# Skip weights of a state-space convolution put into PSUM by TensorE, and a rounding constant put into the instruction

## The chip, the cores and the metric

The kernel runs on one core of one Trainium2 chip. The metric is the device time of one execution in microseconds. Before the change the median of three runs is 1748.3 us (1747.56 to 1751.75). One further execution was profiled; its span, from the first to the last instruction, is 1749.5 us. The engines are called PE (TensorE matmul), PEld (TensorE weight load), DVE (VectorE), ACT (ScalarE), POOL (GpSimd) and SP (SyncE, which here only issues DMAs).

## The reference, cut to what matters

A layer norm with modulation feeds a diagonal state-space convolution, whose result, with a skip term, is added to the input; then a gated MLP follows, which the change does not touch.

```python
def _A_ref(u, A_re, A_im, B_re, B_im, C_re, C_im, log_dt, Dskip):   # L = 2048, D = 576, N = 128
    dt = exp(log_dt)[:, None]
    logdA = dt * (A_re + 1j * A_im);  dB = dt * (B_re + 1j * B_im);  Cc = C_re + 1j * C_im
    P = exp(logdA[:, :, None] * l[None, None, :])
    K = einsum("dn,dnl,dn->dl", Cc, P, dB).real
    y = irfft(rfft(u, 2L) * rfft(K, 2L))[:L] + u * Dskip
x = x + ga * _A_ref(h, ...)          # h: layer norm of x, modulated by c
x = x + gb * _B_ref(h2, ...)         # MLP with a spatial gate
```

The skip term `u * Dskip` is the same as adding `Dskip` to the kernel `K` at lag 0. The kernel before does it in that way.

## The kernel before, in words

The function `ssm` does the convolution part, `Mlp` the rest. The 576 channels are cut into 36 groups of 16 channels. For each group g these units make the convolution kernel in the frequency domain:

- `e_unit` (L442): TensorE makes logarithms of magnitudes in PSUM, ACT takes Exp of them (L449 two banks, L452 one bank) into the tile `et`.
- `t_unit` (L456): TensorE makes phases (L465). For g below NR = 10 TensorE also adds and takes away the rounding constant MAGIC (L469) and DVE copies the result (L477). For the other 26 groups ACT writes phase + MAGIC (L480, `Identity` with the per-partition column `magic` of the tile `consts_s` as bias) and DVE takes the rounded phase from the phase (L481). Then DVE takes the absolute value of the result (L482). All of it is in the tile `ft`.
- `s_unit` (L485): two Sin on ACT (L487, L488), in place.
- `p_unit` (L490): four DVE products of magnitudes and sines (L498 to L501) into `pg` and `et`.
- `kg_unit` (L504): 32 group products on TensorE (L511), 128 x 32 weights against 64 columns, four channels side by side in the four quarters of the output partitions, into one PSUM bank (`pk`, four of them in rotation); ACT copies the bank's 256 columns to the tile `kab` (L514).
- `d_unit` (L516): DVE adds the skip weights of the group to column 63 of each of the four 64-column pieces of `kab` (L518; 128 partitions x 4). The skip weights lie in the tile `dsk`, 4 columns for each group, with a number in partitions 0, 32, 64 and 96 and zeros elsewhere.
- `k1_unit` (L520): eight matmuls (L528) turn `kab` with the constant `r1`, ACT (L535) or DVE (L533) copies the result to `k1`.

When a chunk of 128 channels is complete, `u_unit` (L574: matmul L578, copy L579, two DMAs on POOL L580 and L581), `z_unit` (L584: matmuls L590, DVE product L591), `v_unit` (L594: matmuls L598 and L599, copy L600, DMA L601) and `y_unit` (L637: matmuls L644, DVE add L646, DMA L647) convolve it with the layer-normed input `u`.

The layer norm itself is done early: `ln_load`, `ln_stats` (L389; for the last two of four row blocks with `bn_stats` into the tile `bs`), `ln_rows` (L414) and `ln_half` (L423: matmuls L431, copies to `st1o` L433, which has two buffers, and a DMA on POOL to `u_d` L434). The constant matrices `r1`, `fwd`, `inva`, `invb` and `ones` are views of one tile `small`, which is loaded at the start by SP. The DRAM array `c_small` holds seven 128 x 128 matrices, of which the first is the identity; the kernel before skips it here.

The order: in the early part `early_steps` (L674) records units in the order of a long string, one letter for a unit and a number for its group; from group 9 on, a loop of ticks (L735) records one step of each unit for each tick, in the order of one of three strings (L756). ACT, and after the letters V and T also DVE and TensorE, are not bound to that order: a scheduler moves instructions within each engine. So a change of one unit also moves others. SP and POOL are queues in order.

## Time and profile before

The whole program is bound by TensorE in the MLP (after about 440 us); the convolution, where the change lies, is the first 440 us. Busy time by stage, from the view of busy time by stretch, in us:

| stretch | PE | DVE | ACT | POOL | granted clock |
|---|---|---|---|---|---|
| 0 to 44 | 11.73 | 32.66 | 28.52 | 19.07 | 1.00 |
| 175 to 219 | 43.07 | 41.15 | 42.34 | 14.59 | 0.94 |
| 394 to 438 | 29.68 | 36.89 | 20.74 | 9.68 | 0.84 |
| whole span, 1749.5 | 1654.4 | 1256.1 | 834.3 | 250.5 | 0.982 |

How to read it: an engine that is busy for nearly the whole of a stretch may be what bounds it; in the stretches of 43 or 44 us between 175 and 350 us three engines are, at once. The chain of waits (the work that ended last, followed back) then says which of them set the pace, piece by piece. Matmul ends are modelled in these profiles, so a busy PE need not be PE at its limit. A float32 matmul stands in the trace as two records: 32 group products of one group are 64 records.

### The profile page before, as it was taken

To read this page: it belongs to the slowest core of one execution; us is meant where nothing else is said; L and a number is where in the kernel's file an instruction comes from. 1 tells how busy PE (TensorE), PEld (TensorE's weight loads), DVE (VectorE), ACT (ScalarE), POOL (GpSimd) and SP (SyncE) were. 2 spreads that over 40 slices of the span, in tenths; PEclk is the share of its full clock that TensorE was granted. 3 is DMA by queue.
4 is the path that set the end of the run, shared out by engine and by line. 5 is a ranking of instruction groups with operands and counts; after the bars stand their busy time and mean duration, and the time that the engine had idled before them with its cause. 6 is when DMAs were issued, how large, how long until landed. Compare 5 with 4: busy or idle time off the path is not lost.

```text
span 1749.5 us, 36390 instructions
## 1 busy us (share of the span) xinstructions
PE 1654.4 (95%) x15174; PEld 1241.1 (71%) x15174; DVE 1256.1 (72%) x2259; ACT 834.3 (48%) x1121; POOL 250.5 (14%) x412
## 2 busy tenths in 40 slices
PE   2788999996999999999999999999999999999999
PEld 1344666664455446777878888888888888888887
DVE  7876999948999997888898767797444387334432
ACT  6877999834677665445443433343221233122210
POOL 4421332342122110000000000000111100111100
PEclk9897999998999999999999999999999999999999
DMA  8477656798698798777656887764766563556531
GB/s 227 136 223 229 187 155 170 207 271 248 215 292 272 222 249 290 258 253 261 221 193 205 289 290 263 241 231 138 246 219 231 195 224 106 194 197 208 193 110 41
DMA packets 182934, 376.24 MB, mean 215 GB/s; under 512 B 39105, under 2 KB 102977, under 8 KB 182001
## 3 DMA queue, kind: packets, MB, share of 16 engines
q1 hardware_dynamic: 138304, 168.50, 31.9%
q0 software_dynamic: 37984, 178.55, 31.2%
q10 hardware_dynamic: 6480, 26.86, 3.8%
q8 instruction: 119, 1.95, 0.5%
q14 instruction: 47, 0.38, 0.1%
HBM read 263.11 MB, written 101.31 MB: 208 GB/s over the span
## 4 chain that ended last, share of the span: by engine, by line
PE 32%; issue 28%; DVE 18%; DMA 4%; POOL 3%; ACT 2%; SPq 0%; POOLq 0%; ACTq 0%; DVEq 0%
PE ps L152 28%; POOL zset L1906 2%; DMA zset<-set_d 2%; DVE bsz L152 2%; DVE zset L152 1%; DVE n L152 1%; DVE gt L152 1%; DVE rq L152 1%; DVE wsp L152 1%; PE pk L578 1%; PE pk L598 1%; PE pk L590 1%; DVE pg L499 1%; DVE wso L152 1%; DVE ft L481 1%
## 5 line engine op out<-in xcount | busy, mean ns | idle before, releaser
L152 PEld LDWEIGHTS <-zset 128*128 128x128 f16 x7182 | 701.9, 98 | 92.6 <-DVE zset L152 7.6
L152 PE MATMUL ps<-wsp,zset 128*128 128x256 f16 x6048 | 667.7, 273 | 7.2 <-DVE zset L152 5.8
L152 PE MATMUL pz<-wz,nt 128*128 128x512 f16 (+1 forms) x1120 | 221.9, 358 | 9.0 <-DVE nt L152 4.3
L152 ACT ACTIVATE z<-gt 128x1024 f16<-128x1024 f32 x56 | 59.0, 1054 | 287.0 <-DVE gt L152 287.0
L152 PEld LDWEIGHTS <-nt 128*128 128x128 f16 x1120 | 109.1, 98 | 115.7 <-DVE nt L152 5.8
L1906 POOL DMA_DIRECT2D zset<-set_d x96 | 50.8, 529 | 869.1 <-PE ps L152 619.7
L152 DVE SCALAR_TENSOR_TENSOR gt<-ps,sc,bsp 128x512 f32<-128x512 f32 x36 | 27.0, 750 | 205.5 <-PE ps L152 203.8
L152 PE MATMUL ps<-wout,z 128*128 128x288 f16 x1344 | 170.0, 286 | 0.0
L152 PEld LDWEIGHTS <-z 128*128 128x128 f16 x1344 | 131.5, 98 | 33.0
L152 PE MATMUL ps<-n2o,zset 128*128 128x256 f16 x1134 | 128.2, 273 | 0.0
L152 DVE SCALAR_TENSOR_TENSOR gt<-ps,sc,gt 128x512 f32<-128x512 f32 (+1 forms) x180 | 122.2, 696 | 7.6
L152 DVE TENSOR_TENSOR raw<-raw 128x512 f32<-128x512 f32 (+2 forms) x228 | 119.2, 528 | 11.2 <-DMA raw<-z_d 6.9
L152 ACT ACTIVATE zset<-raw 128x1792 f16<-128x1792 f32 x48 | 81.2, 1691 | 58.3 <-PE ps L152 25.3
L152 DVE TENSOR_TENSOR zset<-raw,zset 128x1792 f16<-128x1792 f32 x48 | 97.0, 2020 | 15.9 <-ACT zset L152 15.9
L152 DVE TENSOR_TENSOR z<-ps,z 128x512 f32<-128x512 f32 (+1 forms) x126 | 72.0, 599 | 36.8 <-ACT z L152 26.7
L152 ACT ACTIVATE wsp<-raw,sc 128x1792 f16<-128x1792 f32 x25 | 44.6, 1785 | 42.7 <-DVE raw L152 35.0
L152 ACT ACTIVATE z<-z,sc 128x1024 f32<-128x1024 f32 x21 | 24.1, 1148 | 75.6 <-DVE z L152 71.9
L152 ACT ACTIVATE z<-pz,sc 128x512 f32<-128x512 f32 (+1 forms) x96 | 52.0, 582 | 16.2 <-DMA z_d<-z 9.8
L152 PE MATMUL ps<-n2q,wf 128*128 128x512 f16 x252 | 55.7, 379 | 0.0
L152 ACT ACTIVATE z<-z,nm,r 128x1152 f32<-128x1152 f32 x24 | 31.5, 1342 | 49.7 <-DVE nm L152 29.3
L152 PE MATMUL ps<-wout,z1b 128*128 128x288 f16 x384 | 52.6, 286 | 0.5 <-ACT z1b L152 0.5
L152 DVE SCALAR_TENSOR_TENSOR wsp<-raw,sc,wsp 128x1792 f16<-128x1792 f32 x25 | 51.9, 2078 | 0.0
(345 smaller groups left out, 2452.7 us busy)
## 6 DMA issues: line engine op xcount, KB each, us to landing
zset<-set_d POOLq DMA_DIRECT2D x96, 896.0 KB, 4.9
raw<-z_d SPq DMA_DIRECT2D x48, 512.0 KB, 5.5
set_d<-zset ACTq DMA_DIRECT2D x24, 896.0 KB, 5.9
z_d<-z POOLq DMA_DIRECT2D x32, 576.0 KB, 9.7
zset<-wa_d POOLq DMA_DIRECT2D x18, 896.0 KB, 4.9
raw<-in_w_spT SPq DMA_DIRECT2D x25, 512.0 KB, 4.4
set_d<-zset SPq DMA_DIRECT2D x12, 896.0 KB, 5.5
u_d<-st1o POOLq DMA_DIRECT2D x16, 576.0 KB, 4.8
```

What stands on the lines that cost most here:

```text
L152: return self.tc.keep_in_program_order(f(*a, **k))
L481: V.scalar_tensor_tensor(f, f, MAGIC, pa, op0=ALU.subtract, op1=ALU.subtract)
L499: V.tensor_tensor(pr, pi, c3[:, :, None, :].to_broadcast([128, 16, 2, 32]), op=ALU.mult)
L578: T.matmul(pm, fwd, u1, start=True, stop=True)
L590: T.matmul(pm[:, w * j:w * j + w], cst[k // 8][:, k % 8], k1t[c][:, k, :w], start=True, stop=True)
L598: T.matmul(pm, inva, zz[:, 0], start=True, stop=False)
L1906: self.nc.gpsimd.dma_start(o, self.set_d[f, j - 1] if j else self.wa_d[f])
```

## The change

Three edits:

1. `d_unit` goes. In its place `kg_unit` begins with four matmuls: the columns of the identity that belong to a quarter of the partitions (128 x 32 weights) against the group's four columns of `dsk`, written to columns 63, 127, 191 and 255 of the bank. They start the accumulation; all group products then accumulate onto them. The identity comes from the first matrix of `c_small`, so `small` has seven matrices in place of six, and its load 128 x 896 numbers in place of 128 x 768. The letters d go from the order strings.
2. L480 becomes `Copy` with the constant MAGIC as a number in the instruction.
3. `bs` has one buffer in place of two.

```diff
-        small = cp.tile([128, 6, 128], F32, name="small")
-        r1 = [small[:, 0], small[:, 1]]
-        fwd, inva, invb, ones = (small[:, i] for i in range(2, 6))
+        small = cp.tile([128, 7, 128], F32, name="small")
+        eye = small[:, 0]
+        r1 = [small[:, 1], small[:, 2]]
+        fwd, inva, invb, ones = (small[:, i] for i in range(3, 7))
...
-                bs = ep.tile([128, 4, 2, 6], F32, name="bs")
+                bs = ep.tile([128, 4, 2, 6], F32, name="bs", bufs=1)
...
-                A.activation(f, pa, AF.Identity, bias=magic)
+                A.activation(f, pa, AF.Copy, bias=MAGIC)
...
         def kg_unit(g):
             pr, pi, gr, gi = tt.pop(g)
             pm = ps1()
+            for j in range(4):
+                rows = slice(32 * j, 32 * j + 32)
+                T.matmul(pm[rows, 63:256:64], eye[:, rows], dsk[:, 4 * g:4 * g + 4], start=True, stop=False, skip_group_check=True)
             for i in range(4):
-                for x_, y_, st in ((gr, pr, True), (gi, pi, False)):
+                for x_, y_, st in ((gr, pr, False), (gi, pi, True)):
                     for j in range(4):
                         c = 4 * i + j
                         T.matmul(pm[32 * j:32 * j + 32, 64 * i:64 * i + 64], x_[:, c], y_[:, c].rearrange("p s j -> p (s j)"),
-                                 start=st, stop=not st, skip_group_check=True)
+                                 start=False, stop=st, skip_group_check=True)
...
-        def d_unit(g):
-            kk = kab[g]
-            V.tensor_tensor(kk[:, :, 63], kk[:, :, 63], dsk[:, 4 * g:4 * g + 4], op=ALU.add)
...
-                    q.dma_start(small, I["c_small"][:, 128:].rearrange("p (i c) -> p i c", i=6))
+                    q.dma_start(small, I["c_small"].rearrange("p (i c) -> p i c", i=7))
...
-            for n in ('kpt1svyzdeeu', 'ktespy1dzvu', 'ktvsdzuyp1')[tick % 3]:
+            for n in ('kpt1svyzeeu', 'ktespy1zvu', 'ktvszuyp1')[tick % 3]:
```

In the whole program DVE has 36 instructions fewer (all of them L518), TensorE 144 matmuls more, and ACT 33 table loads in place of 35. Behind the convolution no instruction stands elsewhere than before. Within it the scheduler moves many. Three places:

ACT in the early part, from the Sin of a group and the layer norm's statistics to the Exp of three groups, before:

```order
L488 ACTIVATE ft<-ft 128x1024
L452 ACT_TABLE_LOAD
L452 ACTIVATE et<-pk 128x512
L218 ACTIVATE pt<-t_ph 128x432
L433 ACTIVATE st1o<-ps 128x576 x2
L487 ACT_TABLE_LOAD
L487 ACTIVATE ft<-ft,consts_s 128x1024
L220 ACTIVATE pt<-t_sq_609 128x432
L433 ACTIVATE st1o<-ps 128x576 x2
L488 ACTIVATE ft<-ft 128x1024
L449 ACT_TABLE_LOAD
```

and now (line numbers are up to three higher, L514 has become L518, and the copy to `k` is still L535):

```order
L489 ACTIVATE ft<-ft 128x1024
L221 ACTIVATE pt<-t_sq_478 128x432
L401 ACTIVATE st1o,ss<-ln_x,nm 128x576
L488 ACTIVATE ft<-ft,consts_s 128x1024
L489 ACTIVATE ft<-ft 128x1024
L219 ACTIVATE pt<-t_ph 128x432
L434 ACTIVATE st1o<-ps 128x576 x2
L518 ACTIVATE kab<-pk 128x256
L221 ACTIVATE pt<-t_sq_613 128x432
L535 ACTIVATE k_923<-pk 128x32x16
L434 ACTIVATE st1o<-ps 128x576 x2
L450 ACT_TABLE_LOAD
```

The single Exp that stood between two groups' Sin has moved to the Exp before them, so two table loads are gone here. A second such pair is gone a little later, and one new pair has come, ahead of six copies to `st1o`:

```order
L535 ACTIVATE k_923<-pk 128x32x16
L453 ACT_TABLE_LOAD
L453 ACTIVATE et<-pk 128x512
L372 ACTIVATE gar<-ps 128x576
L434 ACTIVATE st1o<-ps 128x576 x6
L518 ACTIVATE kab<-pk 128x256
L434 ACTIVATE st1o<-ps 128x576
L488 ACT_TABLE_LOAD
```

DVE in the steady part, the products of two groups (`pg`, `et`) with the phases (`ft`) of others between them, before:

```order
L498 TENSOR_TENSOR pg<-et,ft 128x1024
L499 TENSOR_TENSOR pg<-et,ft 128x1024
L481 SCALAR_TENSOR_TENSOR ft<-ft,ps 128x1024
L500 SCALAR_TENSOR_TENSOR et<-ft,et 128x16x32
L501 TENSOR_TENSOR et<-ft,et 128x16x32
L482 TENSOR_SCALAR ft<-ft 128x1024
L591 TENSOR_TENSOR zz<-pk,uu 128x1024
L518 TENSOR_TENSOR kab<-kab,dsk 128x4
L498 TENSOR_TENSOR pg<-et,ft 128x1024
```

and now:

```order
L499 TENSOR_TENSOR pg<-et,ft 128x1024
L500 TENSOR_TENSOR pg<-et,ft 128x1024 x2
L501 SCALAR_TENSOR_TENSOR et<-ft,et 128x16x32
L502 TENSOR_TENSOR et<-ft,et 128x16x32
L482 SCALAR_TENSOR_TENSOR ft<-ft,ps 128x1024
L533 COPY k_1934<-pk 128x32x16
L483 TENSOR_SCALAR ft<-ft 128x1024
L591 TENSOR_TENSOR zz<-pk,uu 128x1024
L499 TENSOR_TENSOR pg<-et,ft 128x1024
```

The addition L518 is gone; one product of the next group stands ahead of the phase subtraction (now L482), which has moved back behind it and behind the two `et` products.

On TensorE the four new matmuls (L510) stand right ahead of the first group products (L515, before L511). On POOL the six DMA issues of the last pole table (`pa_d`) now stand ahead of the second write of `u_d`, which stood ahead of them; one DMA issue changes places with its neighbours in the steady part, and two reads of `u_d` on SP stand behind a load of MLP weights in place of ahead of it.

4 lines of the change are left out of this document (2 added, 2 removed), and 6 rows, old and new, of the table T.

## The prediction

> **What bounds the kernel now.** Behind 440 us nothing moves, so only the convolution counts, and the question is whether it ends earlier. I read first the view of busy time by stretch (from and to, length, then busy us of PE, PEld, DVE, ACT and POOL with their instructions, granted clock, DMA share, GB/s):
>
> ```profile
> 0.00:44.00 44.00, 11.73 (x49) 4.52 (x50) 32.66 (x107) 28.52 (x55) 19.07 (x36) 1.00 0.86 228
> ...
> 219.00:262.00 43.00, 42.00 (x642) 25.84 (x631) 42.34 (x54) 42.10 (x58) 14.84 (x26) 1.00 0.55 155
> 262.00:306.00 44.00, 43.40 (x656) 27.09 (x655) 42.82 (x55) 41.28 (x56) 12.38 (x21) 1.00 0.61 171
> 306.00:350.00 44.00, 43.56 (x593) 27.30 (x595) 41.63 (x54) 37.84 (x52) 14.10 (x25) 1.00 0.75 206
> 350.00:394.00 44.00, 43.70 (x392) 29.38 (x391) 17.98 (x29) 15.81 (x25) 17.64 (x29) 1.00 0.98 270
> ```
>
> The reader is to see that from 219 to 306 us three engines have hardly 1 to 3 us to spare in 43 or 44, and that after 350 us DVE and ACT have much. So work taken from DVE and ACT and given to PE cannot bring much: the engine that gets it is as full. Which one sets the pace, the chain of waits says (start, us, what; its borders only):
>
> ```profile
> 225.48 1.23 DVE pg L499
> ...
> 280.59 0.68 DVE ft L482
> ...
> 281.93 1.12 PE pk L578 x2
> 283.06 1.10 PE pk L511 x64
> ...
> 296.89 0.69 DVE k L533
> ...
> 325.81 1.12 PE pk L578 x2
> ...
> 360.07 1.03 PE pk L511 x64
> ...
> 377.64 0.88 PE pk L578 x2
> ```
>
> DVE sets the pace from 225 to 281 and from 297 to 325 us, 85 us in all; PE from 281 to 297 and from 325 to 378 us. What follows to 440 us hangs on when the last chunk is ready, and I let it move one to one.
>
> **The skip addition leaves DVE.** DVE in order of time, with one addition and its neighbours (a number in brackets is the idle time ahead, and what ended it); the additions' group from 212 to 325 us; and their two longest waits:
>
> ```profile
> 259.98 1.21 DVE L498 TENSOR_TENSOR pg<-et,ft 128x1024 f32<-128x1024 f32 x1
> 261.11 1.22 DVE L499 TENSOR_TENSOR pg<-et,ft 128x1024 f32<-128x1024 f32 x1
> ...
> 263.57 0.16 DVE L518 TENSOR_TENSOR kab<-kab,dsk 128x4 f32<-128x4 f32 x1
> 263.64 0.69 DVE L646 TENSOR_TENSOR xb<-pk,xb 128x512 f32<-128x512 f32 x1
> 264.24 1.21 DVE L481 SCALAR_TENSOR_TENSOR ft<-ft,ps 128x1024 f32<-128x1024 f32 x1
> ...
> L518 DVE TENSOR_TENSOR kab<-kab,dsk 128x4 f32<-128x4 f32 x16 | 2.6, 160 | 0.0
> ...
> 157.27 0.17 DVE L518 TENSOR_TENSOR kab<-kab,dsk 128x4 f32<-128x4 f32 x1 [1.40 <-ACT kab L514]
> 158.27 1.22 DVE L481 SCALAR_TENSOR_TENSOR ft<-ft,ps 128x1024 f32<-128x1024 f32 x1 [0.83 <-ACT ft L480]
> ...
> 361.59 0.17 DVE L518 TENSOR_TENSOR kab<-kab,dsk 128x4 f32<-128x4 f32 x1 [1.97 <-ACT kab L514]
> ```
>
> An addition lasts 0.16 us, but the next instruction starts 0.07 us behind it (263.57 to 263.64); instructions overlap by their ends, as L646 does, of 0.69 us, whose follower starts after 0.60. So one addition gives back 0.07 us where DVE is full. From 212 to 325 us there are 16, one in 7.1 us; in the 85 us that DVE bounds that makes 12, and 12 x 0.07 = 0.84 us: I take **-0.8**. The bounds are 0 (PE binds in its place) and 12 x 0.16 = 1.9 us. The waits bring nothing: at 157 us DVE waits again right after, 0.83 us for the phase copy, and at 361 us PE bounds and DVE is free more than half of the time (17.98 of 44 us busy). The addition was also a station between `kab` and its matmuls L528; taking it out makes `kab` ready earlier, but the group products are a tick ahead of L528, so nobody waited for it there.
>
> **Four matmuls more on TensorE for each group.** No operation of 4 columns stands in this stage, so the nearest rows are the group products themselves, eight records (four matmuls) at a step, and what comes next:
>
> ```profile
> 329.43 0.29 PE L511 MATMUL pk<-pg 128*32 128x64 f32 x8
> 329.54 0.29 PE L511 MATMUL pk<-et,pg 128*32 128x64 f32 x8
> ...
> 329.98 0.29 PE L511 MATMUL pk<-et,pg 128*32 128x64 f32 x8
> 330.21 0.39 PE L448 MATMUL ps<-sel,lb 48*128 48x512 bf16 x2
> ```
>
> A step of four products takes 0.11 us (329.43 to 329.54). The new step loads weights of the same shape and has four columns in place of 64. Below it costs nothing, where PE waits for the products' operands anyhow; above it costs what the change to another kind of matmul takes, 0.23 us (329.98 to 330.21). I take 0.11, since its four weight loads are those of the products and only the columns are fewer. The Trainium skill, "TensorEngine Tiling (Array Packing)", section "Instruction Overhead", has a rule that speaks against this edit: a matmul over one column takes as long as one over some 60. By it a step costs 0.11 us again; without it, in proportion to columns, 0.007. No row here decides that.
>
> On the chain, group products stand seven times in the stretches that PE bounds, the first at 283.06 and the last at 360.07 us: 7 x 0.11 = **+0.8**, with bounds 0 and 7 x 0.23 = 1.6. So the edit's two halves cancel: what DVE gives back in its stretches PE takes in its own. The bank's first matmul now comes earlier than the products' operands, so a bank is held longer, but in the steady order the four stand right ahead of the products.
>
> **The constant in the instruction.** ACT, groups from 212 to 325 us:
>
> ```profile
> L487 ACT ACTIVATE ft<-ft,consts_s 128x1024 f32<-128x1024 f32 x16 | 18.5, 1155 | 1.3 <-DVE ft L482 1.2
> L480 ACT ACTIVATE ft<-ps,consts_s 128x1024 f32<-128x1024 f32 x16 | 18.1, 1131 | 0.0
> L488 ACT ACTIVATE ft<-ft 128x1024 f32<-128x1024 f32 x16 | 16.9, 1058 | 0.0
> ```
>
> The two Sin differ in that one reads a column as bias: 1155 against 1058 ns, 97 ns. L480 reads such a column too, so 26 copies save up to 26 x 0.097 = 2.5 us of ACT. ACT is not what bounds from 225 us on; the cover is DVE's and PE's work, and only some two copies ahead of 225 us lie on the path: **-0.2**, bounds 0 and -2.5. Were the other two quicker, ACT with 42.10 of 43 us would be next.
>
> **What the scheduler moves.** In the early part two ACT table loads go, net of the pair that comes. ACT there, then the waits where the new pair lands, and what POOL and the DMAs do:
>
> ```profile
> 67.42 1.04 ACT L488 ACTIVATE ft<-ft 128x1024 f32<-128x1024 f32 x1
> 68.48 1.28 ACT L452 ACT_TABLE_LOAD   x1
> 69.78 0.60 ACT L452 ACTIVATE et<-pk 128x512 f32<-128x512 f32 x1
> ...
> 71.92 1.28 ACT L487 ACT_TABLE_LOAD   x1
> ...
> 85.50 0.65 ACT L433 ACTIVATE st1o<-ps 128x576 f32<-128x576 f32 x1 [1.66 <-PE ps L431]
> ...
> 134.47 1.19 ACT L433 ACTIVATE st1o<-ps 128x576 f32<-128x576 f32 x2 [2.65 <-DMA u_d<-st1o]
> ...
> 138.08 0.65 ACT L433 ACTIVATE st1o<-ps 128x576 f32<-128x576 f32 x1 [2.41 <-PE ps L431]
> ```
>
> ```profile
> 76.20 0.76 POOL L434 DMA_DIRECT2D u_d<-st1o  x1 [3.06 <-ACT st1o L433]
> 76.95 3.73 POOL L152 DMA_DIRECT2D pa_d<-pt  x6
> ...
> small<-in_c_small SPq DMA_DIRECT2D x1, 384.0 KB, 3.3
> ...
> u_d<-st1o POOLq DMA_DIRECT2D x16, 576.0 KB, 4.8
> ```
>
> The first pair (68.48 and 71.92) lies where ACT runs without a gap: 2 x 1.28 = 2.56 us less there. From 85 us on ACT waits for PE, so I pass on half: **-1.3**, bounds 0 and -2.6. The second removed pair and the new one lie where ACT waits 2.65 and 2.41 us for others, which hides them; uncovered, the new one costs 2.56. The Trainium skill, "ScalarE: Activation LUTs", section "What ACT_TABLE_LOAD costs", adds to each switch a drain of 1.38 us; by it the pair would be worth an estimated 2 x (1.28 + 1.38) = 5.3 us, and the half of it 2.7. The trace differs: the load starts 0.02 us behind L488's end and Exp 0.02 us behind the load's.
>
> The second write of `u_d`, at 76.20 us, now stands behind six issues of 3.73 us. Its buffer of `st1o` is wanted again at 85.50 us; the write lands 4.8 us after issue, so at 81.0, and 3.7 us later at 84.7, 0.8 us in time: nothing. The load of `small` grows by a sixth, 64 KB, at 228 GB/s 0.28 us; the loads behind it queue, but DVE and ACT are busy for only 32.66 and 28.52 of the 44 us there and take up part of it: **+0.1**. One buffer for `bs` costs nothing, since DVE alone writes and reads it, in order. The reads of `u_d` behind weights on SP are some ticks ahead of their use.
>
> The sum: -0.8 + 0.8 - 0.2 - 1.3 + 0.1 = **-1.4 us**. The profiled execution's span is 1749.5 us, 1.2 above the median of the runs shown; 1749.5 - 1.4 = 1748.1 in span is 1746.9 in the runs' terms.
>
> **Rivals.** *Everything removed pays* (faster): the whole pair, -2.6, all 26 phase copies, -2.5, and DVE's -0.8 with PE's step at nothing: -5.8 with the load's 0.1, so 1742.5 us. For it speaks that ACT is busy 42.10 of 43 us, so its time may matter on the way to DVE; against it that the chain there is DVE and PE. *PE takes over the conv stage* (slower): if a step costs the change of kind, 0.23 us, and PE is really full from 212 us on, then 16 groups to 325 us and five after it pay, 21 x 0.23 = 4.8 us, DVE's saving vanishes into waiting, and with +0.1 the time is 1753.2; it decides above some 0.15 us a step. PE's 43.40 of 44 us speak for it, the modelled ends and the chain against. *The new order costs* (slower): DVE now does a product (1.13 us from start to start, 259.98 to 261.11) ahead of the phase subtraction, which frees the two PSUM banks that Exp's matmuls wait for; if PE then waits once in three ticks, from 225 to 325 us five times, that is 5 x 1.13 = 5.7 us, with PE's 0.8 about 1754.5. Against it: DVE is in order and full, so a product done early is not done later. *The constant's edit does nothing*, since a copy with a number is no shorter than with a column: 0.2 us, within the forecast.
>
> **How the numbers follow.** A measurement of this kernel can tell about 0.3%, 5.2 us, from no change. I give the forecast (no change that can be told, 1746.9) and what lies about it 0.62, the faster rival 0.22, PE's takeover 0.07, and the new order 0.09. The range 1740 to 1753 us leaves out about a tenth on each side: below, some of the faster rival with more waits gone; above, the two slower ones, which begin at its end. So faster by over 0.3% has 0.22, within 0.3% 0.63, slower 0.15; the last 0.01 is the slower rivals' short of the border.
>
> **What would show it.** Right: 33 table loads, of which none between 65 and 75 us; the last group products 0 to 3 us earlier; the phase copies near 1035 ns; the new step at 0.1 us from its start to the products'; busy DVE some 5.8 us (36 x 0.16) lower; the chain with more PE from 225 to 325 us. Wrong: a step above 0.2 us; DVE waiting for PE's products by more than 0.5 us a tick; `st1o` copies waiting for the write of `u_d` near 85 us; or the six copies near 130 us late by the new pair.

## The result, and the profile after

The changed kernel is slower. Its median was 1763.48 us over four runs (1761.30 to 1764.79), the kernel before beside it 1750.03 us over four (1747.56 to 1753.91): a ratio of 1.0070, with a 95% interval of 1.0051 to 1.0089. Repeated later, beside the experiments, it was 1760.97 us against 1754.25, 1.0044 (1.0027 to 1.0062). The two intervals overlap; between them the loss is 7 to 13 us, where 1.4 us of gain was predicted. The profiled execution spans 1762.0 us.

The view of busy time by stretch, of the changed kernel, in the stretches shown of before (from and to, length, busy us of PE, PEld, DVE, ACT and POOL with their instructions, granted clock, DMA share, GB/s):

```profile
219.00:262.00 43.00, 41.91 (x675) 26.08 (x674) 41.69 (x48) 40.88 (x56) 14.83 (x26) 1.00 0.49 143
262.00:306.00 44.00, 42.30 (x697) 26.57 (x697) 40.62 (x48) 40.86 (x55) 12.24 (x21) 1.00 0.58 170
306.00:350.00 44.00, 42.61 (x612) 25.83 (x612) 39.61 (x45) 38.05 (x52) 12.24 (x22) 1.00 0.65 188
350.00:394.00 44.00, 43.48 (x481) 29.20 (x478) 21.51 (x25) 14.32 (x24) 18.93 (x31) 1.00 0.94 244
```

Between 262 and 350 us PE is busy for 84.91 us, where it was for 86.96; DVE for 80.23, where it was for 84.45. PE has more work now, and yet is idle for longer: something keeps all of them waiting. It isn't the clock: the granted clock was 1.00 in these four stretches, before and after. After 350 us DVE has 3.5 us more to do than before: work came late. The groups of one line and shape, of the changed kernel from 212 to 330 us, say who waits (busy us, mean ns | idle us ahead, and for what):

```profile
L482 DVE SCALAR_TENSOR_TENSOR ft<-ft,ps 128x1024 f32<-128x1024 f32 x17 | 20.6, 1214 | 2.1 <-ACT ft L481 2.0
L488 ACT ACTIVATE ft<-ft,consts_s 128x1024 f32<-128x1024 f32 x17 | 19.6, 1155 | 3.0 <-DVE ft L483 2.7
L481 ACT ACTIVATE ft<-ps 128x1024 f32<-128x1024 f32 x17 | 17.6, 1038 | 0.0
L510 PE MATMUL pk<-dsk,small 128*32 128x4 f32 x128 | 3.9, 183 | 1.2 <-DVE zz L591 1.2
```

and the phase subtraction of the kernel before, in the same view from 212 to 325 us:

```profile
L481 DVE SCALAR_TENSOR_TENSOR ft<-ft,ps 128x1024 f32<-128x1024 f32 x16 | 19.5, 1217 | 0.3 <-ACT ft L480 0.2
```

DVE and ACT wait for each other. DVE's phase subtraction now waits 2.1 us for ACT's copy, where it waited 0.3; ACT's Sin waits 3.0 us for DVE's absolute values (L483), where it waited 1.3. The place can be read off ACT in order of time. Before:

```profile
278.70 0.59 ACT L600 ACTIVATE v<-pk 128x512 f32<-128x512 f32 x1
279.31 1.28 ACT L449 ACT_TABLE_LOAD   x1
280.61 1.02 ACT L449 ACTIVATE et<-ps 128x1024 f32<-128x1024 f32 x1
```

and in the changed kernel:

```profile
283.50 0.60 ACT L600 ACTIVATE v<-pk 128x512 f32<-128x512 f32 x1
285.95 1.15 ACT L488 ACTIVATE ft<-ft,consts_s 128x1024 f32<-128x1024 f32 x1 [1.85 <-DVE ft L483]
287.11 1.28 ACT L450 ACT_TABLE_LOAD   x1
288.41 1.02 ACT L450 ACTIVATE et<-ps 128x1024 f32<-128x1024 f32 x1
```

The scheduler has moved one Sin of the next group ahead of the Exp table load. From the copy `v` to the first Exp it was 1.91 us (278.70 to 280.61) and is 4.91 us (283.50 to 288.41). The Sin saves no table load: its partner (L489) still needs the one that follows. What it waits for stands on DVE:

```profile
282.96 1.21 DVE L482 SCALAR_TENSOR_TENSOR ft<-ft,ps 128x1024 f32<-128x1024 f32 x1
284.09 1.22 DVE L499 TENSOR_TENSOR pg<-et,ft 128x1024 f32<-128x1024 f32 x1
285.23 0.68 DVE L483 TENSOR_SCALAR ft<-ft 128x1024 int32<-128x1024 int32 x1
```

and who waits for the late Exp, on PE:

```profile
289.48 0.28 PE L466 MATMUL ps<-sel,lc 48*128 48x256 bf16 x2 [0.62 <-ACT et L450]
...
290.89 0.39 PE L449 MATMUL ps<-sel,lb 48*128 48x512 bf16 x2 [0.54 <-ACT et L450]
```

The phase matmuls need the two PSUM banks that Exp frees; the phase copy comes late behind them, and with it the phase subtraction. A second such Sin stands on the chain of waits of the changed kernel (start, us, what):

```profile
331.74 1.15 ACT ft L488
332.90 1.28 ACT L450
335.71 0.92 ACT et L450
```

The first one is not itself on that chain, but two of the Exp copies behind it are (289.33 and 290.71 us). In the whole program these are the first Sin of groups 27 and 33; no other Sin of the loop of ticks stands ahead of an Exp table load. My prediction showed the move of a product on DVE, but not this one on ACT.

### The profile page after: what moved, and what is told of

Same layout as the page of the kernel before. It is cut to its first block, busy times and chain, and to the rows that moved or that the text cites. A ratio compares the mean times of both kernels' runs of the same rounds, so it can differ in the third digit from the quotient of the medians.

```text
span 1762.0 us, 36913 instructions
## 1 busy us (share of the span) xinstructions
PE 1664.9 (94%) x15462; PEld 1247.6 (71%) x15462; DVE 1253.5 (71%) x2223; ACT 831.1 (47%) x1119; POOL 249.2 (14%) x412
## 4 chain that ended last, share of the span: by engine, by line
PE 64%; DVE 16%; DMA 7%; issue 6%; ACT 5%; POOL 1%; SPq 1%; ACTq 0%; DVEq 0%; POOLq 0%
PE ps L152 55%; DMA zset<-set_d 2%; DVE bsz L152 1%; DVE zset L152 1%; PE pk L515 1%; DVE rq L152 1%; DVE n L152 1%; PE pk L528 1%; PE pk L578 1%; PE pk L598 1%; DVE wsp L152 1%; PE pk L590 1%; DMA wst<-in_w_in 1%; DVE gt L152 1%; DMA u_d<-st1o 1%
## 5 line engine op out<-in xcount | busy, mean ns | idle before, releaser
L152 PEld LDWEIGHTS <-zset 128*128 128x128 f16 x7182 | 702.8, 98 | 95.2 <-DVE zset L152 7.2
L152 PE MATMUL ps<-wsp,zset 128*128 128x256 f16 x6048 | 669.2, 273 | 9.0 <-DVE zset L152 5.5
L152 PE MATMUL pz<-wz,nt 128*128 128x512 f16 (+1 forms) x1120 | 222.3, 358 | 11.0 <-DVE nt L152 4.4
L152 ACT ACTIVATE z<-gt 128x1024 f16<-128x1024 f32 x56 | 59.0, 1054 | 283.3 <-DVE gt L152 283.3
L152 PEld LDWEIGHTS <-nt 128*128 128x128 f16 x1120 | 108.9, 98 | 118.1 <-DVE nt L152 5.8
L152 DVE SCALAR_TENSOR_TENSOR gt<-ps,sc,bsp 128x512 f32<-128x512 f32 x36 | 27.0, 750 | 207.8 <-PE ps L152 206.1
L152 PE MATMUL ps<-wout,z 128*128 128x288 f16 x1344 | 170.0, 286 | 0.0
L152 PEld LDWEIGHTS <-z 128*128 128x128 f16 x1344 | 131.5, 98 | 33.0
L152 PE MATMUL ps<-n2o,zset 128*128 128x256 f16 x1134 | 128.2, 273 | 0.0
L152 DVE SCALAR_TENSOR_TENSOR gt<-ps,sc,gt 128x512 f32<-128x512 f32 (+1 forms) x180 | 122.2, 696 | 7.6
L152 DVE TENSOR_TENSOR raw<-raw 128x512 f32<-128x512 f32 (+2 forms) x228 | 119.1, 528 | 11.3 <-DMA raw<-z_d 7.0
L152 ACT ACTIVATE zset<-raw 128x1792 f16<-128x1792 f32 x48 | 81.2, 1691 | 62.6 <-PE ps L152 33.5
L152 DVE TENSOR_TENSOR zset<-raw,zset 128x1792 f16<-128x1792 f32 x48 | 96.9, 2020 | 15.6 <-ACT zset L152 15.6
L152 DVE TENSOR_TENSOR z<-ps,z 128x512 f32<-128x512 f32 (+1 forms) x126 | 72.0, 599 | 36.8 <-ACT z L152 26.7
L152 ACT ACTIVATE wsp<-raw,sc 128x1792 f16<-128x1792 f32 x25 | 44.6, 1785 | 42.7 <-DVE raw L152 35.0
L152 ACT ACTIVATE z<-z,sc 128x1024 f32<-128x1024 f32 x21 | 24.1, 1148 | 75.6 <-DVE z L152 71.9
L152 ACT ACTIVATE z<-z,nm,r 128x1152 f32<-128x1152 f32 x24 | 31.5, 1342 | 54.2 <-DVE nm L152 30.9
L152 ACT ACTIVATE z<-pz,sc 128x512 f32<-128x512 f32 (+1 forms) x96 | 51.5, 582 | 10.3 <-DMA z_d<-z 6.4
L152 PE MATMUL ps<-n2q,wf 128*128 128x512 f16 x252 | 55.7, 379 | 0.0
L152 PE MATMUL ps<-wout,z1b 128*128 128x288 f16 x384 | 52.4, 286 | 0.0
L500 DVE TENSOR_TENSOR pg<-et,ft 128x1024 f32<-128x1024 f32 x36 | 43.7, 1219 | 12.1 <-ACT ft L488 9.4
```

The costliest lines, as they stand in the source:

```text
L152: return self.tc.keep_in_program_order(f(*a, **k))
L500: V.tensor_tensor(pr, pi, c3[:, :, None, :].to_broadcast([128, 16, 2, 32]), op=ALU.mult)
```

## Experiments

Single executions of the same kernel differ by as much as the effect (beside the experiments, runs of the kernel before lay between 1744.76 and 1760.71 us), so besides the ratios I use a measure inside each profile: the times from the first copy to `gsp` to the `kab` of group 16, from there to the `kab` of group 24, and from there to the last addition `xb`. Its border rows, for the kernel before:

```profile
276.49 0.36 ACT L514 ACTIVATE kab<-pk 128x256 f32<-128x256 f32 x1
...
399.79 0.67 DVE L152 TENSOR_TENSOR xb<-pk,xb 128x512 f32<-128x512 f32 x1
```

and for the changed kernel:

```profile
281.20 0.36 ACT L518 ACTIVATE kab<-pk 128x256 f32<-128x256 f32 x1
...
408.77 0.68 DVE L152 TENSOR_TENSOR xb<-pk,xb 128x512 f32<-128x512 f32 x1
```

that is 123.3 and 127.6 us. All kernels (each row one profile, in us; the ratio to runs of the kernel before that were taken beside it, with its 95% interval). The experiments ran in five sets, each on another chip. The column "9 to last `xb`" begins at the `kab` of group 9, the tenth, as several expectations do:

| kernel | start to `gsp` | to `kab` 16 | 16 to 24 | 24 to last `xb` | 9 to last `xb` | ratio |
|---|---|---|---|---|---|---|
| before, first profile | 57.6 | 162.5 | 56.3 | 123.3 | 231.7 | |
| before_again | 54.4 | 163.0 | 56.3 | 123.2 | 231.8 | 0.9996 (0.9979 to 1.0013) |
| const_only | 58.5 | 159.3 | 56.0 | 124.4 | 231.6 | 1.0012 (1.0000 to 1.0024) |
| no_addition | 57.5 | 160.3 | 56.0 | 123.4 | 231.7 | 1.0008 (0.9993 to 1.0023) |
| larger_load | 59.6 | 162.6 | 56.3 | 123.2 | 229.8 | 1.0027 (1.0011 to 1.0043) |
| skip_only | 59.5 | 160.8 | 57.2 | 128.5 | 236.2 | 1.0044 (1.0028 to 1.0061) |
| after, first profile | 61.3 | 163.1 | 56.8 | 127.6 | 236.0 | 1.0070 (1.0051 to 1.0089) |
| after_again | 58.0 | 162.5 | 56.8 | 127.1 | 235.7 | 1.0044 (1.0027 to 1.0062) |
| pinned_before | 59.9 | 162.0 | 55.3 | 123.9 | 231.7 | 1.0009 (0.9994 to 1.0024) |
| pinned_after | 59.5 | 165.2 | 55.3 | 126.4 | 233.5 | 1.0033 (1.0019 to 1.0047) |
| sin_moved | 58.7 | 163.7 | 55.3 | 126.1 | 232.2 | 1.0023 (1.0010 to 1.0037) |
| step_added | 59.7 | 166.2 | 55.5 | 124.5 | 231.0 | 1.0032 (1.0014 to 1.0050) |
| step_twice | 59.6 | 163.9 | 55.8 | 126.2 | 236.5 | 1.0032 (1.0011 to 1.0054) |
| step_single | 57.0 | 165.8 | 56.2 | 126.3 | 238.6 | 1.0042 (1.0022 to 1.0063) |
| step_less | 58.3 | 160.0 | 54.8 | 123.1 | 228.5 | 0.9979 (0.9960 to 0.9997) |
| step_behind | 60.6 | 169.3 | 55.2 | 126.9 | 234.5 | 1.0031 (1.0012 to 1.0051) |
| fixed_before | 60.1 | 186.1 | 76.7 | 145.5 | 286.5 | 1.0392 (1.0370 to 1.0415) |
| fixed_after | 60.0 | 182.5 | 76.4 | 141.4 | 283.3 | 1.0371 (1.0351 to 1.0391) |
| fixed_step_added | 58.0 | 192.0 | 76.9 | 144.8 | 287.9 | 1.0401 (1.0377 to 1.0424) |
| fixed_step_twice | 59.1 | 188.5 | 76.5 | 145.2 | 287.7 | 1.0393 (1.0378 to 1.0409) |

The first profiles of the two kernels differ by 12.6 us in span: 3.6 at the start, 0.6 up to `kab` 16, 4.7 from there to the last `xb` and 3.6 behind it. The second profiles differ by 5.2 us: 3.6, -0.5, 4.3 and -2.2. The early part and the loop, from `kab` 16 to the last `xb`, repeat within each kernel to 0.6 us, and the loop's loss is the one that comes both times and is larger than that; the start of one kernel varies by 3 us (57.6 and 54.4).

The borders 16 and 24 are later than the expectations, which name others, and the results differ by it. A stretch from `kab` 9 takes in the first ticks of the loop, which depend on how the early part ended: larger_load, whose loop is that of the kernel before, is 1.7 us shorter from `kab` 9 to 12 and level with it to 0.1 us from there on. And one border moves with the place of its copy in ACT's order: in const_only `kab` 24 is 1.1 us early and `kab` 25 level again. So the last two stretches, 16 to 24 and 24 to the last `xb`, say most when they are added.

**One part alone.** Four kernels: the constant without the rest; the skip matmuls with the old constant; the kernel before with the addition left out; and the kernel before with the larger load and one buffer for `bs`.

```diff
# const_only: before, and
-                A.activation(f, pa, AF.Identity, bias=magic)
+                A.activation(f, pa, AF.Copy, bias=MAGIC)
# skip_only: after, and
-                A.activation(f, pa, AF.Copy, bias=MAGIC)
+                A.activation(f, pa, AF.Identity, bias=magic)
# no_addition: before, and
-            V.tensor_tensor(kk[:, :, 63], kk[:, :, 63], dsk[:, 4 * g:4 * g + 4], op=ALU.add)
+            pass
# larger_load: before, and (the views of small, its load and bufs=1 of bs as in the change)
-        small = cp.tile([128, 6, 128], F32, name="small")
+        small = cp.tile([128, 7, 128], F32, name="small")
...
```

> The kernel before with the second edit alone: the phase copy takes its constant as a number. Addition on DVE and everything else as before. Theory O (the scheduler's new order costs, and it comes from the four matmuls and the larger load): 1745 to 1751 us, since few instructions change places here; the copy L480 near 1035 ns in place of 1131. Theory P (TensorE's added work costs): the same, 1746 to 1750. Theory C (the second edit costs, by the order it brings in the steady part): 1755 to 1763.

> The change without its second edit: the skip weights are added by TensorE, the phase copy keeps its column as bias. Theories O and P: 1759 to 1766 us, as the changed kernel or 0 to 3 us above it. Theory C: 1746 to 1752.

> The kernel before with the addition on DVE left out and nothing in its place, so the skip term is missing from the result. The order of the rest hardly changes. Theories O and P: 1746 to 1750 us, 0 to 2 less than before, since DVE gets back 0.07 us for each addition and the order stays. If leaving the addition out were itself what costs (by the order that DVE and ACT take without it), 1755 to 1763.

> The kernel before with seven matrices in the load of small and one buffer for bs, and no other edit: the identity is loaded and not used. The scheduler reorders the early part for it (37 table loads in place of 35). Theory O: 1751 to 1757 us, the copies to st1o 2 to 5 us later from 130 us on, the steady part shifted by the same amount and not more. Theory P: 1748 to 1751, no place later by more than 1 us.

The skip matmuls alone lose what the whole change loses when repeated, 1.0044, and most of their loss lies behind group 24 (128.5 us); over both stretches of the loop they lose 6.1 us, more than the whole change does (4.7), for a reason that these runs don't show. Skip_only also has the two Sin ahead of the Exp table load; const_only, no_addition and larger_load have none, and their loops lose 0.7 us or less. Leaving the addition out gives 0.3 us from 16 to 24 and loses 0.1 behind: it was off the path. The constant costs or gains nothing that the times tell: 0.7 us more in the two stretches of the loop together, nothing from `kab` 9. The larger load leaves the three stretches from `gsp` to the last `xb` as they were, to 0.1 us. Yet its ratio, 1.0027, lies clear of 1: 2 to 7 us, where I had forecast 0.1. In its profile the start is longer, by 2.0 us against the first profile of before, and that is within what the same kernel shows (57.6 and 54.4); where the loss comes from is not in these columns.

**Both kernels again, and with Exp and Sin pinned.** Pinning keeps the Exp of groups from 9 on and the Sin of groups from 8 on in the order in which the program names them.

```diff
# pinned_before and pinned_after, in e_unit (the other Exp too); in s_unit the two Sin alike, with g >= 8
...
-            A.activation(e[:, 1024:], pb, AF.Exp)
+            A_ = mlp.tied.scalar if g >= 9 else A
...
+            A_.activation(e[:, 1024:], pb, AF.Exp)
```

> The kernel before, unchanged, to have its profile from the same chip as the other runs. By the reading that the stretch of the MLP's first transfers (500 to 520 us) takes back gains of the convolution, this profile, which is of a kernel with no change at all, has a wait of 4 to 7 us there that the first profile of it (span 1749.5 us) lacked, and its span is about 1754 us. By the rival, that the wait belongs to the changed kernels, it has none and its span is about 1750 us.

> The changed kernel, unchanged, timed beside the others. If its parts add up it takes 1.0044 (matmuls for the addition) plus 0.0012 (constant in the instruction), about 1.006 of the kernel before, 1765 us where that takes 1755. If the first comparison held an extra of its own, it comes out near 1.0044, that is no more than with the first edit alone.

> The changed kernel, with the Exp and Sin activations of the loop of ticks (groups 8 and 9 on) kept in the order in which the program names them, so that no Sin can be moved ahead of the Exp table load of the next tick. Theory O (the scheduler's new order costs: a Sin stands ahead of the table load, waits there for VectorE's absolute values, and the Exp copies and with them TensorE come late): the two steps of about 2.5 us each near 285 and 335 us go, and the ratio falls from 1.006 to about 1.003 or less. Theory P (TensorE's added steps cost, 36 of 0.1 to 0.2 us on its path): nothing changes, 1.006. Theory L (the early part, before 130 us, sets the loss): a late start of the convolution of 3 us stays, 1.002 to 1.006.

> The kernel before with the same Exp and Sin activations kept in program order, the control for the run on the changed kernel. Theory O: the kernel before had no Sin ahead of a table load, so nothing is gained, ratio 0.999 to 1.001. If the pinning itself speeds the loop, this one falls as much as the changed kernel does with it, to about 0.997.

The changed kernel repeats its loop to 0.5 us (56.8 and 127.6, 56.8 and 127.1), the kernel before to 0.1. With the pins the loss behind group 24 is 2.5 us (126.4 against 123.9), without them 3.9 to 4.3; over both stretches of the loop it is 2.5 against 4.3 to 4.8. So some 2 us go, as theory O has it, and a part stays. From 16 to 24 the pins gain 1.0 us in the kernel before and 1.5 in the changed one, and in the kernel before 0.6 of it is lost again behind, so the comparison must be of pinned with pinned. The ratios alone don't settle it: the intervals of pinned_after (1.0033) and after_again (1.0044) overlap. Before_again lost 2.5 us against the first profile between 500 and 520 us, not the 4 to 7 expected, and its span was 1749.7 us, not 1754.

**The step itself.** All pinned: the step issued twice; one matmul with the whole identity in place of four quarters; the step added to the kernel before with the addition kept; and one of the eight steps of group products left out.

```diff
# step_twice: pinned_after, and
-            for j in range(4):
-                rows = slice(32 * j, 32 * j + 32)
-                T.matmul(pm[rows, 63:256:64], eye[:, rows], dsk[:, 4 * g:4 * g + 4], start=True, stop=False, skip_group_check=True)
+            for x in range(2):
+                for j in range(4):
+                    rows = slice(32 * j, 32 * j + 32)
+                    T.matmul(pm[rows, 63:256:64], eye[:, rows], dsk[:, 4 * g:4 * g + 4], start=not x, stop=False, skip_group_check=True)
# step_single: pinned_after, and in its place
+            T.matmul(pm[:, 63:256:64], eye, dsk[:, 4 * g:4 * g + 4], start=True, stop=False, skip_group_check=True)
# step_less: pinned_before, and
-                for x_, y_, st in ((gr, pr, True), (gi, pi, False)):
+                for x_, y_, st in ((gr, pr, True), (gi, pi, False))[:1 if i == 3 else 2]:
```

> The changed kernel with Exp and Sin pinned, and the new step (four matmuls of four columns) issued twice for each group; the skip weights are thus added twice. Measured in the profile from the second product zz (181 us in the kernel before) to the last copy v (394 us), where the kernel before needs 213 us, and the pinned changed kernel 3.0 us more. Theory P (TensorE sets the pace in every tick, so each of the 28 steps in this stretch is paid in full at some 0.11 us): about 6 us more than before. Theory O (only the order costs): 3.0 us more as with one step. My prediction's reading (seven steps on the path): 3.0 plus 0.8.

> The changed kernel with Exp and Sin pinned, and one matmul with the whole identity (128x128 weights, four columns) in place of the four with a quarter each. Theory P with the cost in the weight loads and instructions: a quarter of the instructions, 1 us or less more than before in the stretch of the convolution instead of 3.0. Theory P with the cost in the change between kinds of matmul (full array to quarters): 3 us or more, up to 28 x 0.23 = 6.4.

> The kernel before with Exp and Sin pinned, the larger load of small matrices, and the new step of four matmuls added in front of the group products, while VectorE's addition stays; the skip weights are added twice. Theory P: 3 us more than before in the stretch of the convolution, as in the pinned changed kernel, so the step alone carries it. Theory D (taking the addition from VectorE gives something back there): more than in the pinned changed kernel, 3.0 + 0.8 or above. Theory O: 0 to 0.5 us.

> The kernel before with Exp and Sin pinned, and one of the eight steps of group products (the last four matmuls, 64 columns each) left out for each group; the last quarter of the taps lacks the imaginary part. Theory P: about 28 x 0.11 = 3 us less than before in the stretch of the convolution. If VectorE or ScalarE set the pace in most ticks, as my prediction read the chain (seven steps on the path): 0.8 us less or nothing.

From group 16 to group 24, where no Sin is out of place in any of these kernels, eight groups take 55.3 us pinned without the step, 55.5 with the step added, 55.3 in the pinned changed kernel, 55.8 with two steps and 54.8 with a step of products less. So a step of four columns costs 0.00 to 0.06 us a group and one of 64 columns gives back 0.07: theory P, with 0.1 a group in all of them, would have given 0.8. Behind group 24 the step added to the pinned kernel before costs 0.6 us, while the pinned changed kernel, with the same step, loses 2.5: the step is not most of what it loses.

That comparison is a clean one: from 200 us on the order of step_added is that of pinned_before on ACT, on TensorE but for the step, and on DVE but for one row. Over both stretches, twenty groups, the step costs 0.8 us there, and the step of products left out gives back 1.4, 0.07 a group in all of them: more than my seven steps allowed. From the second `zz` to the last `v`, the stretch that the expectations name, it is 213.5 us in pinned_before and 215.6 in pinned_after, 216.0 with the step doubled, 217.8 with the single matmul, 213.9 with the step added and 211.2 with a step of products less. So doubling costs 0.4 us, where my prediction had 0.8 and theory P 3; for the step left out, 2.2 us less than pinned_before and 1.5 less than the kernel before, neither the 0.8 of my reading nor theory P's 3 is right.

The single matmul is the worst, 0.9 us over the four quarters in eight groups. Its profile shows it (TensorE in order of time):

```profile
233.44 0.38 PE L510 MATMUL pk<-dsk,small 128*128 128x4 f32 x2
233.76 0.32 PE L515 MATMUL pk<-pg 128*32 128x64 f32 x8
233.90 0.29 PE L515 MATMUL pk<-et,pg 128*32 128x64 f32 x8
```

The products start 0.32 us behind it; in the changed kernel, with four quarters, 0.09 us:

```profile
229.29 0.24 PE L510 MATMUL pk<-dsk,small 128*32 128x4 f32 x8
229.38 0.30 PE L515 MATMUL pk<-pg 128*32 128x64 f32 x8
229.49 0.29 PE L515 MATMUL pk<-et,pg 128*32 128x64 f32 x8
```

In the ratios neither doubling nor adding the step can be told from pinned_after (1.0032, 1.0032 and 1.0033); step_added has most of its own in the early part (166.2 against 162.0 us), where its other instructions also changed places.

**The order held the same.** In these four every matmul and VectorE operation of the loop, and its Exp and Sin, stand in program order, so the loop's order differs by the edits alone.

```diff
# fixed_before and fixed_after: pinned_before and pinned_after, and in the loop of ticks
+            if tick == 9:
+                V, T = mlp.tied.vector, mlp.tied.tensor
```

> The kernel before, with every matmul, every VectorE operation and every Exp and Sin of the loop of ticks kept in program order, so that edits can be compared with the order of TensorE, VectorE and ScalarE held the same. It is the reference of the next three; the program's order is not the scheduler's, so its own time may be some us longer. Measured: from the copy kab of the tenth group to the last addition xb (231.7 us in the kernel before, 235.7 to 236.0 in the changed kernel).

> The changed kernel with the same pins; in the loop it differs from the fixed kernel before by its own edits alone, on no engine by the order. Theory O (the scheduler's new order costs in the loop, the edits themselves next to nothing): within 1.5 us of the fixed kernel before in that stretch. Theory P (TensorE's step costs in every tick): 28 steps of 0.08 to 0.11 us, 2.2 to 3.1 us more, less what the addition and the copies give back.

> The kernel before with the same pins, with the new step in front of the group products and VectorE's addition kept (the skip weights are added twice). Theory P: 2.2 to 3.1 us more than the fixed kernel before. Theory O: less than 1 us more. The difference to the fixed changed kernel is what the addition and the constant in the instruction give back: 0.8 + 0.2 us by my prediction, nothing if both are off the path.

> The fixed changed kernel with the step issued twice per group (the skip weights are added twice). Theory P: another 2.2 to 3.1 us over the fixed changed kernel. Theory O: less than 1 us over it. By my prediction's seven steps: 0.8.

Program order is 70 us slower, so this loop isn't full as the real one is, and it can only answer in part. From 16 to 24 all four agree to 0.5 us, in no order of their work. Over the whole stretch the changed kernel is not slower than the kernel before but 4.4 us faster behind group 16 (217.8 against 222.2), and the second step gives that back (221.8). A step that costs nothing from 16 to 24 and 3.8 us behind 24 fits neither theory; TensorE was granted 0.94, 0.96, 0.93 and 0.91 of its clock from 240 to 380 us in these four, in the order of the table, and 1.00 in pinned_before, so I read no price from the stretch behind 24 here. These four decide nothing between the theories; for the step, with the order held in a full loop, it is step_added that answers.

**Two Sin moved, no work added.** The kernel before, pinned, with the first Sin of groups 27 and 33 named ahead of the Exp of the next ticks, where the scheduler put them in the changed kernel. Behind these two places the scheduler moves other rows too: counted at their old and their new place, 4 on ACT, 18 on DVE and 18 on TensorE, among them a product of the next group on DVE that now stands ahead of the `et` products.

```diff
# sin_moved: pinned_before, and in the loop of ticks
                 if n == "e":
+                    if tick in (27, 33) and tick not in ahead:
+                        ahead.add(tick)
+                        s_unit(tick, second=False)
                     for g in exps:
...
+                elif n == "s" and tick - 1 in ahead:
+                    s_unit(tick - 1, first=False)
```

> The kernel before with Exp and Sin pinned, in which just two Sin (the first of the pair of groups 27 and 33) are issued ahead of the Exp of the next ticks, as the scheduler put them in the changed kernel; no work is added or taken away. Measured from the copy kab of the tenth group to the last addition xb: 231.7 us in the pinned kernel before. Theory O: two steps of 2 to 3 us at the two places (some 280 and 330 us), together 4 to 5 us, which is the loss of the changed kernel in this stretch (4.2 us). Theory P: nothing, 231.7, since TensorE has no new work.

ACT of pinned_before at that place, in order of time (pinned instructions all have line L152):

```profile
280.70 0.60 ACT L602 ACTIVATE v<-pk 128x512 f32<-128x512 f32 x1
281.32 1.28 ACT L152 ACT_TABLE_LOAD   x1
282.82 1.02 ACT L152 ACTIVATE et<-ps 128x1024 f32<-128x1024 f32 x1 [0.21 <-PE ps L448]
```

and of sin_moved, first ACT, then the two waits on TensorE:

```profile
281.21 0.60 ACT L604 ACTIVATE v<-pk 128x512 f32<-128x512 f32 x1
282.95 1.15 ACT L152 ACTIVATE ft<-ft,consts_s 128x1024 f32<-128x1024 f32 x1 [1.15 <-DVE ft L483]
284.12 1.28 ACT L152 ACT_TABLE_LOAD   x1
285.42 1.02 ACT L152 ACTIVATE et<-ps 128x1024 f32<-128x1024 f32 x1
```

```profile
286.49 0.29 PE L466 MATMUL ps<-sel,lc 48*128 48x256 bf16 x2 [0.35 <-ACT et L152]
287.89 0.39 PE L448 MATMUL ps<-sel,lb 48*128 48x512 bf16 x2 [0.54 <-ACT et L152]
```

From `v` to the first Exp it is 4.21 us in place of 2.12, and TensorE waits for the same two banks as in the changed kernel. Up to group 24 nothing changes (55.3 and 55.3); behind it the two Sin cost 2.2 us (126.1 against 123.9). Where it begins, the `kab` copies show, of groups 24 and 25 in pinned_before:

```profile
277.20 0.38 ACT L516 ACTIVATE kab<-pk 128x256 f32<-128x256 f32 x1 [0.29 <-PE pk L513]
...
286.07 0.43 ACT L516 ACTIVATE kab<-pk 128x256 f32<-128x256 f32 x1
```

and in sin_moved:

```profile
277.71 0.38 ACT L518 ACTIVATE kab<-pk 128x256 f32<-128x256 f32 x1 [0.29 <-PE pk L515]
...
288.67 0.43 ACT L518 ACTIVATE kab<-pk 128x256 f32<-128x256 f32 x1
```

From `kab` 12 to 24 the two kernels keep step to 0.02 us; from 24 to 25 it is 10.96 us in place of 8.87, 2.1 more. One group on, half of that is back, as the Sin that was done early is missing behind the next table load; the rest of the 2.2 comes later. That the moves cost this is shown, the two Sin together with what the scheduler moved behind them; it is half of the 4 to 5 us that theory O expected. By the stretch that the expectation names, from `kab` 9, it is 232.2 against 231.7 us, since sin_moved takes 1.7 us less up to `kab` 12, as larger_load does. The ratios, 1.0023 and 1.0009, point the same way as the profiles, but their intervals overlap. Here the absolute values follow the subtraction after a copy of 0.68 us; in the changed kernel a product of 1.22 us stands between them, and the Sin waits 1.85 us in place of 1.15.

**The step behind the products.** The pinned changed kernel, with the four matmuls last.

```diff
# step_behind: pinned_after, and the four matmuls behind the loop over i
-                T.matmul(pm[rows, 63:256:64], eye[:, rows], dsk[:, 4 * g:4 * g + 4], start=True, stop=False, skip_group_check=True)
+                T.matmul(pm[rows, 63:256:64], eye[:, rows], dsk[:, 4 * g:4 * g + 4], start=False, stop=True, skip_group_check=True)
```

> The pinned changed kernel with the new matmuls behind the group products instead of in front of them, so that no PSUM bank is taken before the products' operands are there; the sum is the same. Theory B (in the early groups the step in front takes a bank some tens of matmuls early and holds up the rest): from the copy gsp to the kab of the tenth group 108 to 110 us instead of 113.5, the loop as in the pinned changed kernel (233.5 us from there to the last xb). Theory P: the loop unchanged at 233.5. Theory O: the early part moves by an amount that no bank explains, in either direction, since other instructions change places there too.

The early part gets longer, 169.3 us in place of 165.2 (116.9 in place of 113.5 to the `kab` of the tenth group, where theory B had 108 to 110), and the loop stays to 0.5 us (55.2 and 126.9). So theory B's forecast failed. As other instructions changed places here too (35 table loads against 31), it is not shown what a PSUM bank taken early costs. Over all kernels with the normal order that part lies between 159.3 and 169.3 us, with no side for the changed kernel (163.1 and 162.5) against the kernel before (162.5 and 163.0).

## Why the prediction was wrong, point by point

- **What bounds the loop**: right in that three engines are full at once; but I drew from it only that work moved from one to another brings little. It also means that a wait of 2 us on any of them can be paid. And I took too much from the chain of waits. Between its borders at 225 and 281 us it leaves DVE for 13 us, over TensorE, ACT, POOL and a DMA:

```profile
238.38 1.10 PE pk L511 x64
...
240.91 0.47 POOL uu L580
...
247.96 2.66 DMA v_d<-v
```

  so DVE's two stretches had 72 us, not 85. From 225 to 325 us the chain's pieces on PE add up to 16 us before, 48 in the changed kernel and 79 in pinned_before, whose loop is as fast as that of the kernel before. In a loop with three full engines the chain does not say what a step costs, and my twelve additions and seven steps were counted along it.
- **The addition leaves DVE (-0.8)**: too large. Left out alone it brings 0.2 us from group 16 to the last `xb`. DVE's busy time fell by 2.6 us in the whole program (1256.1 to 1253.5), 36 x 0.07, as the term had an addition, but the row "busy lower by 5.8" was wrong.
- **Four matmuls more (+0.8)**: right in size, and partly by luck: the step takes 0.09 us where I took 0.11; added to the pinned kernel before, it costs 0.2 us over eight groups and 0.6 behind them, 0.8 in all, but spread over twenty groups at 0.04 and not over seven at 0.11. The Trainium skill, "TensorEngine Tiling (Array Packing)", section "Instruction Overhead", says that one column takes as long as some 60. The trace agrees but for some hundredths: from one start to the next it is 0.09 us for four columns and 0.11 for 64, where in proportion it would be 0.007. The rival *PE takes over the conv stage* falls by its price, since it needed 0.15 us a step.
- **The constant (-0.2)**: the copies went to 1038 ns, as forecast (1035); no gain followed in const_only, as it would be with ACT's time there covered.
- **What the scheduler moves (-1.3)**: the step that failed, in two ways: the pair of table loads brought nothing, and the loop's new order, which I put at nothing, cost at least 2.2 us. There are 33 table loads, and none between 65 and 75 us; ACT's next one there is now

```profile
78.45 1.28 ACT L450 ACT_TABLE_LOAD   x1
...
128.11 1.28 ACT L453 ACT_TABLE_LOAD   x1
...
137.90 1.19 ACT L434 ACTIVATE st1o<-ps 128x576 f32<-128x576 f32 x2 [2.57 <-DMA u_d<-st1o]
```

  so 2.6 us of ACT's time is gone, and the early part is as long as before (163.1 and 162.5 against 162.5 and 163.0): nothing of it is passed on. The new pair at 128.11 us costs nothing either, as I said; the copies still wait, 2.57 us for a DMA where it was 2.65. And I priced the loop's new order at nothing, having counted only the table loads and shown one move on DVE; I did not go through ACT's order to the end, where a Sin stands ahead of an Exp table load at two places. The loop lost 4.3 to 4.8 us; the step has 0.8 of it, and moving the two Sin alone costs 2.2.
- **The larger load (+0.1)**: too small by the times, 2 to 7 us for larger_load, which also has one buffer for `bs` and another early order; the cause is open. The nine profiles with seven matrices and the normal order reach `gsp` at 57.0 to 61.3 us, mean 59.4; the seven with six at 54.4 to 59.9, mean 57.8. But the same kernel gave 57.6 and 54.4, and 61.3 and 58.0.
- **Behind the convolution nothing moves**: holds within the scatter. From the last `xb` to the end of the span it is 1349.7 and 1352.7 us before, 1353.3 and 1350.5 after.
- **What would have shown it**: of the four signs that I named for a wrong forecast none came in its form. The step is not above 0.2 us, and DVE doesn't wait for TensorE's products but for ACT's copies, 2.1 us in 17 ticks, far less than 0.5 us a tick. Of the signs for a right forecast four came (the table loads, the copies, the step, more PE in the chain), though the time went the other way: they stand for the terms that I had, not for the one that I lacked. I had no sign for ACT waiting for DVE ahead of a table load.
- **The rivals**: the nearest was *The new order costs*, slower, 1754.5 us (its terms add up to 1754.8), to which I gave a chance of 0.09. Its end is right, PE waiting for the banks that Exp frees, and its product ahead of the phases has a part in it (between subtraction and absolute values); but the wait begins on ACT, at two places, not in every third tick. Against it I held that DVE, in order and full, does not do a product later that it does early. That argument asks only how much work there is; what matters is who waits for the instruction that now comes second.

The sum as measured: from group 16 to 24 0.5 us, from 24 to the last `xb` 3.9 to 4.3 us, together 4.3 to 4.8 of the 6.7 us between the medians of the repeated comparison. The two Sin, with what moves behind them, account for 2.2 us, and the pins, which hold them back, take away as much; the step accounts for 0.8. The other 1.5 us or so are not isolated: with Exp and Sin pinned 2.5 us stay, 1.7 more than the step. Pinned_after still has products of the next group ahead of `zz` on DVE at two late places, which neither pinned_before nor step_added has, and near them it falls behind, by 0.5 us at `kab` 25 and 0.9 at `kab` 31; whether that is the rest was not tried. Also open are the remaining 2 us between the medians, where the larger load's 2 to 7 us are a rival that no profile places, and the 7 us more of the first comparison.

No version beat the kernel before: step_less, which is quicker, leaves out work that is needed.

## What to carry to other kernels

Where a scheduler orders the instructions, an edit has two prices: its own, read from durations, and that of the order it causes, which here was the larger: 2.2 us for two moved Sin, 0.8 for the added step. Look at the new order engine by engine to the end of the stage; the rows to look for are instructions now ahead of a table load or of another change of state, and what they wait for. To separate the prices, force the suspected move into the old kernel with no work added, and add the work to the old kernel with the order held.

## What the runs showed of the hardware that I had not expected

- One matmul with 128 x 128 weights and four columns holds up the following quarter-array products by 0.32 us, four with 128 x 32 weights by 0.09 us (0.315 and 0.084 in the median of all groups): fewer instructions took longer.
- The Exp table load in the changed kernel starts 0.01 us behind the Sin (285.95 + 1.15 = 287.10, then 287.11), and Exp 0.02 us behind its end (288.39, then 288.41). The Trainium skill, "ScalarE: Activation LUTs", section "What ACT_TABLE_LOAD costs", adds a drain of 1.38 us to a switch; the trace differs here too.
- When the first weights of the MLP arrive varies from execution to execution. The kernel before waits for them, in order of time on ACT:

```profile
507.93 1.06 ACT L152 ACTIVATE wsst<-wsst 128x1024 f32<-128x1024 f32 x1 [2.46 <-DMA wsst<-in_w_spT]
```

  and no_addition, which ended the convolution 2.5 us earlier (397.25 against 399.79 us):

```profile
509.61 1.06 ACT L152 ACTIVATE wsst<-wsst 128x1024 f32<-128x1024 f32 x1 [5.83 <-DMA wsst<-in_w_spT]
```

  so a gain of 2 or 3 us in the convolution need not be seen at the end. Before_again, which ended the convolution 2.8 us earlier than the first profile, waited there twice, 2.46 and 2.32 us, and its span came out 0.2 us longer, not shorter. That a gain is always taken back there is not shown.
